# GpSimd instead of VectorE makes the four sums of each decoded w_out group

## The chip, the cores and the metric

The kernel runs on one core of one Trainium2 chip. The metric is the device time of one execution in microseconds (us), and the median of several executions is compared. The engines are called as the profile calls them: PE (TensorE matmuls) with PEld (its weight loads), DVE (VectorE), ACT (ScalarE), POOL (GpSimd) and SP (SyncE, which here only issues DMAs).

## The reference

Sigmoid attention over 8 batches, 12 heads, 448 positions and head size 64, and then a feed-forward layer with erf-gelu over the 3584 tokens (768 to 2048 to 768):

```python
scores = scale * np.matmul(q, k.transpose(0, 1, 3, 2)) - np.log(S)
attn = 1.0 / (1.0 + np.exp(-scores))
x = np.matmul(attn, v)          # then heads side by side: [3584, 768]
...
h = x @ w_in
g = 0.5 * h * (1.0 + erf(h * inv_sqrt2))
return (g @ w_out).astype(np.float32)
```

## The kernel before

**Arithmetic.** Both matrix products of the feed-forward layer are done by a Strassen-like scheme with 7 products of blocks instead of 8 (p = 1 to 7). Each fp32 operand is split in a high part (a rounded copy) and a low part (the rest), and each product is three matmuls: low weight with high operand, high with low, high with high (`terms`, L764). A weight is split by ACT (high, L321) and DVE (low, L328, in `low_to`). The operand of the first layer (x) is split by ACT (L811, L840 and others) and DVE (`combine`, L801, output `xl_p` or `x`); that of the second layer by ACT (L811) and DVE (L801, output `op`).

**Weights.** They are decoded from their memory layout in chunks by the class `Decoder`: ACT makes `me` from `raw` (L149, L160), DVE joins and rounds (`join` L179 and L187, `round` L193) into a tile `wd`. Sixteen chunks are of w_in, the last twelve of w_out; two chunks make one of six w_out groups (0 to 5). For each group `post` makes two sums (L217, L218) and stores five blocks to memory (L220), and `close` makes two differences (L228) and stores them (L229). Nineteen chunks are decoded during attention; the other nine, and all the group sums, fall into the beginning of the feed-forward part. A `wd` tile has two buffers, so the tile of group 2 takes the one of group 0, and its first `join` can only start when every store of group 0 has been read out:

```python
self.out = sb.tile([P, 4 * QUAD], F32, tag="wd", name=f"wd{i}", bufs=2)
```

The stored blocks come back as weight units: SP loads 128 x 768 pieces (`load_to`, L310) into four staging buffers `wst_all`, ACT and DVE split them into `whl`, of which there are four. A unit feeds 18 matmuls. There are 224 units: for each of four batch pairs b 28 of w_in and 28 of w_out.

**Order.** The schedule is written out by hand (`manual_schedule`): each engine runs its instructions in the order in which the program issues them. First comes attention; `last_pair` ends it and runs the decoder up to the sums of group 0. Then `ffn1` of b = 0 walks 56 items, two to a unit, in the order `IN_ORDER`: p = 1 and 2 (items 0 to 15), then 6, 7 and 4 (items 16 to 39), then 5 and 3 (40 to 55). Around each item it issues a share of the decoder's steps and, at fixed items, the splits of x, as the low part for p = 4 behind item 19, whose first user is item 21. `ffn2` of b = 0 follows, with the units of w_out in the order p = 1, 5, 2, 6, 3, 7, 4 and a split of `op` for each unit. `close` of a group is called at least five items after its `post`; for groups 4 and 5 it is called in `ffn2`.

**Queues.** POOL issues the stores of `wd` (L220, L229), the stores of attention's results (L604, L609) and the later loads of x (L353), one behind another in program order.

Of the kernel before, what the change touches and what calls it, by code (L numbers as in the profile page):

```python
# [15 lines left out]
ALU = mybir.AluOpType  # L16
# [6 lines left out]
def tile_sigmoid_attention_gelu_ffn(  # L23
# [10 lines left out]
    nc = tc.nc  # L34
# [69 lines left out]
    def mix(a, s):  # L104
        a11, a12, a21, a22 = a
        s1, s2, s3, s4 = s
        nc.vector.tensor_tensor(s1, a21, a22, op=ALU.add)
        nc.vector.tensor_tensor(s2, s1, a11, op=ALU.subtract)
        nc.vector.tensor_tensor(s3, a11, a21, op=ALU.subtract)
        nc.vector.tensor_tensor(s4, a12, s2, op=ALU.subtract)  # L110
        return {1: a11, 2: a12, 3: s4, 4: a22, 5: s1, 6: s2, 7: s3}
# [10 lines left out]
    def square(m):  # L122
        return m.rearrange("p (h f n) -> p h f n", h=2, f=2)

    class Decoder:
# [77 lines left out]
        def post(self):  # L203
            some = bool(self.mixing or self.pending and self.second)
            while self.mixing:
                j, a = self.mixing.pop()
                quads = [t[:, i * OP : i * OP + OP] for t in (a, self.mixed) for i in range(4)]
                parts = mix(quads[:4], quads[4:])
                for p in (1, 2, 4, 5, 6, 7, 3):
                    n = IN_ORDER.index((p, j))  # L210
                    nc.gpsimd.dma_start(scr_in[n // 2][:, n % 2], parts[p])
                self.done += 1
            while self.pending and self.second:
                (c, e), a = self.pending.pop(0)
                a11, a12, a21, a22 = (a[:, i * QUAD : i * QUAD + QUAD] for i in range(4))
                s2 = self.second(c * KE + e)
                nc.vector.tensor_tensor(a21, a21, a22, op=ALU.add)  # L217
                nc.vector.tensor_tensor(s2, a21, a11, op=ALU.subtract)  # L218
                for p, part in ((2, a12), (4, a22), (1, a11), (5, a21), (6, s2)):
                    nc.gpsimd.dma_start(scr_out[p, c][:, :, :, e], square(part))  # L220
                self.open.append((c, e, a12, a22, s2))
                self.groups += 1
            return some

        def close(self):
            c, e, a12, a22, s2 = self.open.pop(0)
            for p, part in ((3, a12), (7, a22)):
                nc.vector.tensor_tensor(part, part, s2, op=ALU.subtract)  # L228
                nc.gpsimd.dma_start(scr_out[p, c][:, :, :, e], square(part))  # L229
            self.closed += 1  # L230

# [534 lines left out]
    def feed_forward(banks):  # L766
# [110 lines left out]
        def ffn1(b, g, xs):  # L877
# [11 lines left out]
            for n, (p, j) in enumerate(IN_ORDER):  # L889
# [17 lines left out]
                if p == 1:  # L907
                    later.append(lambda g21=g21, ph=ph: nc.scalar.copy(g21, ph))  # L908
                elif p == 2:
                    later.append(lambda g11=g11, ph=ph: gelu(g11, ph))  # L910
                elif p == 6:
                    later.append(lambda g12=g12, ph=ph: nc.scalar.copy(g12, ph))
                elif p == 7:
                    later.append(lambda g22=g22, ph=ph: nc.scalar.copy(g22, ph))
                elif p == 4:
                    later.append(lambda g21=g21, ph=ph: gelu(g21, ph))
                else:
                    dst = g22 if p == 5 else g12
                    h = tmp()
                    combine(h, ph, dst, add)  # L920

                    def close(p=p, r=r, h=h, dst=dst, t1=g[0, 1][c], g11=g[0, 0][c]):
                        gelu(dst, h)
                        if p == 3 and r == 1:
                            later.append(lambda: combine(t1, t1, g11))

                    later.append(close)
# [181 lines left out]
```

## Time and profile before

| | |
|---|---|
| time, median of 3 runs | 1005.85 us (1005.49 to 1006.02) |
| profiled execution: time / span | 1007.21 us / 1005.4 us |
| PE busy | 1000.4 us of the span (99%), 6436 matmuls |
| DVE busy | 719.4 us (72%) |
| ACT busy | 678.2 us (67%) |
| POOL busy | 129.8 us (13%) |
| granted clock of PE | 1.0 of full speed in all 40 slices |

The span is the time from the first to the last instruction of the program; the profiled execution took 1.8 us more than it, and 1.4 us more than the median of the runs. Shares are means over stages: attention ends near 239 us, `ffn1` of b = 0 near 334 us, and the rest repeats four times with no decoding in it. Within 236 to 350 us DVE does the decoder's work beside the splits, and it is there that the change lies.

### The profile page before, as it was taken

The numbers are of one execution on the slowest core, as the hardware profiler recorded it, in microseconds if no ns is written. First come the engines' busy times: TensorE is split into PE (matmuls) and PEld (weight loads), VectorE is DVE, ScalarE is ACT, GpSimd is POOL, SyncE is SP. The second block draws the span as 40 slices with busy tenths as digits, with TensorE's granted clock in tenths as the row PEclk, the third lists the DMA queues.
The fourth block names the chain that finished last, engine by engine and source line by source line (L and its number), as shares of the span: only waits on it lengthen the run. The fifth ranks groups of instructions, "written<-read, shape, count | busy, mean of one in ns | idle before, by whom it ended". The sixth has DMA issues, their size and how long they took to land.

```text
span 1005.4 us, 16639 instructions
## 1 busy us (share of the span) xinstructions
PE 1000.4 (99%) x6436; PEld 901.1 (90%) x6436; DVE 719.4 (72%) x829; ACT 678.2 (67%) x942; POOL 129.8 (13%) x180
## 2 busy tenths in 40 slices
PE   9999999999999999999999999999999999999998
PEld 5665665566999999999999999999999999999998
DVE  3688888888988987764378877535887774378873
ACT  5788888789886665567665655766656467665653
POOL 0234444413223300010000000100000000000000
PEclk9999999999999999999999999999999999999999
DMA  9989999997996665563434446534444543334541
GB/s 270 269 278 337 360 353 348 364 311 264 350 328 212 204 220 145 174 212 126 138 111 131 149 138 190 183 111 137 126 118 147 167 147 115 111 110 126 143 138 67
DMA packets 82928, 199.18 MB, mean 198 GB/s; under 512 B 9120, under 2 KB 33984, under 8 KB 82848
## 3 DMA queue, kind: packets, MB, share of 16 engines
q1 hardware_dynamic: 69360, 152.24, 49.5%
q0 software_dynamic: 11552, 39.23, 11.2%
q10 hardware_dynamic: 1936, 6.63, 2.0%
q8 instruction: 51, 0.84, 0.3%
q14 instruction: 29, 0.24, 0.1%
HBM read 156.10 MB, written 41.29 MB: 196 GB/s over the span
## 4 chain that ended last, share of the span: by engine, by line
PE 93%; DMA 2%; DVE 2%; ACT 1%; issue 1%; DVEq 0%; ACTq 0%
PE pf L764 73%; PE pav L546 11%; PE sc L510 7%; PE sc_t L530 2%; DMA raw<-w_out_dram 1%; DMA wst_all<-scr_in 1%; DVE whl L328 1%; PE sc L498 1%; DMA qk<-k_dram 0%; ACT a_all L471 0%; DVE wd L179 0%; ACT me L149 0%; DVE x L608 0%; ACT whl L321 0%; DVE x L801 0%
## 5 line engine op out<-in xcount | busy, mean ns | idle before, releaser
L764 PE MATMUL pf<-op,whl 128*128 128x448 f32 (+1 forms) x2022 | 382.3, 352 | 0.0
L764 PEld LDWEIGHTS pf<-op,whl 128*128 128x128 f32 x2022 | 381.3, 189 | 0.5 <-DVE op L801 0.2
L764 PE MATMUL pf<-xh_p,whl 128*128 128x448 f32 x1296 | 353.2, 353 | 0.1
L328 DVE TENSOR_TENSOR whl<-wst_all,whl 128x768 fp32r<-128x768 f32 x224 | 213.7, 955 | 153.7 <-ACT whl L321 153.4
L321 ACT CAST whl<-wst_all 128x768 fp32r<-128x768 f32 x224 | 185.9, 830 | 142.7 <-PE pf L764 124.5
L764 PEld LDWEIGHTS pf<-xh_p,whl 128*128 128x128 f32 x1296 | 244.9, 189 | 1.6 <-issue 0.7
L764 PE MATMUL pf<-xl_p,whl 128*128 128x448 f32 x624 | 219.9, 352 | 0.0
L801 DVE TENSOR_TENSOR op<-g,op 128x896 fp32r<-128x896 f32 x112 | 121.5, 1086 | 0.9 <-ACT op L811 0.9
L764 PEld LDWEIGHTS pf<-xl_p,whl 128*128 128x128 f32 x624 | 117.9, 189 | 0.1
L811 ACT CAST op<-g 128x896 fp32r<-128x896 f32 x112 | 104.8, 936 | 1.7 <-PE pf L764 1.7
L546 PE MATMUL pav<-a_all,v 64*64 64x448 f32 x816 | 95.0, 539 | 0.0
L546 PEld LDWEIGHTS pav<-a_all,v 64*64 64x64 f32 x816 | 34.4, 133 | 42.0 <-issue 35.0
L801 DVE TENSOR_TENSOR g<-g,g 128x896 f32<-128x896 f32 x64 | 69.5, 1085 | 0.0
L798 ACT ACTIVATE g<-tmp 128x448 f32<-128x448 f32 x64 | 40.2, 630 | 38.1 <-DVE tmp L801 38.0
L798 ACT ACTIVATE g<-pf 128x448 f32<-128x448 f32 x64 | 34.7, 543 | 39.8 <-PE pf L764 39.5
L353 POOL DMA_DIRECT2D x<-scr_x x24 | 18.3, 815 | 324.5 <-ACT g L908 204.4
L471 ACT ACTIVATE a_all<-sc 128x896 f32<-128x896 f32 x64 | 55.5, 923 | 5.8 <-PE sc L498 3.5
L801 DVE TENSOR_TENSOR tmp<-pf,g 128x448 f32<-128x448 f32 x64 | 39.8, 623 | 26.2 <-PE pf L764 18.7
L546 PE MATMUL pav<-wst_all,v 64*64 64x448 f32 x272 | 55.3, 536 | 0.0
L471 ACT ACTIVATE a_all<-sc_t 128x896 f32<-128x896 f32 x24 | 22.1, 920 | 29.6 <-PE sc_t L530 29.6
L546 PE MATMUL pav<-a_lent,v 64*64 64x448 f32 x192 | 40.5, 537 | 0.0
L458 DVE TENSOR_TENSOR lo_all<-qk,hi_all 128x896 fp32r<-128x896 f32 x34 | 38.1, 1122 | 0.3
(106 smaller groups left out, 1023.2 us busy)
## 6 DMA issues: line engine op xcount, KB each, us to landing
wst_all<-scr_in SPq DMA_DIRECT2D x112, 384.0 KB, 3.2
wst_all<-scr_out SPq DMA_DIRECT2D x112, 384.0 KB, 3.1
v<-v_dram SPq DMA_DIRECT2D x48, 256.0 KB, 9.8
raw<-w_in_dram SPq DMA_DIRECT2D x16, 767.8 KB, 8.4
out_dram<-tmp SPq DMA_DIRECT2D x47, 224.0 KB, 2.1
qk<-q_dram SPq DMA_DIRECT2D x23, 448.0 KB, 9.2
qk<-k_dram SPq DMA_DIRECT2D x46, 224.0 KB, 9.2
scr_out<-wd POOLq DMA_DIRECT2D x36, 256.0 KB, 5.1
```

The lines of the kernel that those rows point to most:

```text
L321: nc.scalar.copy(hl[:, 0], t)
L328: nc.vector.tensor_tensor(hl[:, 1], t, hl[:, 0], op=ALU.subtract)
L353: queue.dma_start(dst[:, :, a], src[:, :, a])
L458: nc.vector.tensor_tensor(lo, raw, hi, op=ALU.subtract)
L471: nc.scalar.activation(to, sc, AF.Sigmoid, bias=NEG_LOG_S, scale=SCALE)
L510: nc.tensor.matmul(sc[:, j], ks[1][rows(j), keys], braid(qs[0][rows(j)]), start=n == 0, stop=n == 2,)
L530: nc.tensor.matmul(sc[rows(p), j], raw[rows(j), p, 1, FULL * P :], raw[rows(j), p, 0], start=True, stop=True,)
L546: nc.tensor.matmul(pav[rows(j), p], vals[u][half, p, j, c], a[p][half, j], start=not swap and c == order[0], stop=c == (order[-1], FULL - ...
L764: nc.tensor.matmul(bank, a, braid(m if half is None else straight(m)[:, half]), **flags)
L798: nc.scalar.activation(straight(dst), unbraid(src), AF.Gelu)
L801: nc.vector.tensor_tensor(out, a, b, op=op)
L811: nc.scalar.copy(op[:, 0], src)
```

## The change

The four additions and subtractions of each group, 24 in all, each 128 partitions x 512 fp32 elements with both inputs in SBUF, are issued on POOL instead of DVE:

```diff
                 s2 = self.second(c * KE + e)
-                nc.vector.tensor_tensor(a21, a21, a22, op=ALU.add)
-                nc.vector.tensor_tensor(s2, a21, a11, op=ALU.subtract)
+                nc.gpsimd.tensor_tensor(a21, a21, a22, op=ALU.add)
+                nc.gpsimd.tensor_tensor(s2, a21, a11, op=ALU.subtract)
                 for p, part in ((2, a12), (4, a22), (1, a11), (5, a21), (6, s2)):
                     nc.gpsimd.dma_start(scr_out[p, c][:, :, :, e], square(part))
...
             for p, part in ((3, a12), (7, a22)):
-                nc.vector.tensor_tensor(part, part, s2, op=ALU.subtract)
+                nc.gpsimd.tensor_tensor(part, part, s2, op=ALU.subtract)
                 nc.gpsimd.dma_start(scr_out[p, c][:, :, :, e], square(part))
```

On POOL, around the end of attention, the stores of group 0 stood behind two stores of attention's results (L609), with the sums elsewhere. Rows of before, in program order (`wd_2386` is the tile of group 0, `s_0` its second sum):

```order
L609 DMA scr_x<-x_0_2764 128x448
L609 DMA scr_x<-x_1_2767 128x448
L220 DMA scr_out_0_97<-wd_2386 512x1x128
L220 DMA scr_out_0_101<-wd_2386 512x1x128
L220 DMA scr_out_0_95<-wd_2386 512x1x128
L220 DMA scr_out_0_103<-wd_2386 512x1x128
L220 DMA scr_out_0_105<-s_0_2781 512x1x128
L609 DMA scr_x<-x_0_2810 128x448
L609 DMA scr_x<-x_1_2813 128x448
L229 DMA scr_out_0_99<-wd_2386 512x1x128
L229 DMA scr_out_0_107<-wd_2386 512x1x128
```

The same place of POOL's program now, without the middle of the stores:

```order
L609 DMA scr_x<-x_1_2767 128x448
L217 ISA
L217 TENSOR_TENSOR wd_2386<-wd_2386 128x512
L218 TENSOR_TENSOR s_0_2781<-wd_2386 128x512
L220 DMA scr_out_0_97<-wd_2386 512x1x128
...
L609 DMA scr_x<-x_1_2813 128x448
L228 TENSOR_TENSOR wd_2386<-wd_2386,s_0_2781 128x512
L229 DMA scr_out_0_99<-wd_2386 512x1x128
L228 TENSOR_TENSOR wd_2386<-wd_2386,s_0_2781 128x512
L229 DMA scr_out_0_107<-wd_2386 512x1x128
L217 TENSOR_TENSOR wd_2594<-wd_2594 128x512
```

Every store of a group now stands behind its sums on POOL, and there is one row that the source does not name: `L217 ISA`, which the built program calls a reload of GpSimd's library of routines (index 0). It stands once, ahead of the first sum.

On DVE, in the first items of `ffn1`, the rows around the first `join` of group 2 (`wd_2975`) change like this (`wd_2594` is the tile of group 1, `whl` the weight units, `xl_p` a low part of x):

```order
 L801 TENSOR_TENSOR xl_p_2955<-x_p_2614,xh_p_2893 128x1344
-L217 TENSOR_TENSOR wd_2594<-wd_2594 128x512
-L218 TENSOR_TENSOR s_1_2967<-wd_2594 128x512
 L179 SCALAR_TENSOR_TENSOR wd_2975<-raw_2544,me_2927 128x1024
```

What is left of DVE's program keeps its order, so a low part (L328) that stood behind a `join` still stands behind it. ACT, SP and PE have the same rows in the same order.

## Rows read from the trace of the kernel before

**Rows 1.** The page: busy time of PE, and its granted clock by slice.
```profile
PE 1000.4 (99%) x6436; PEld 901.1 (90%) x6436; DVE 719.4 (72%) x829; ACT 678.2 (67%) x942; POOL 129.8 (13%) x180
...
PEclk9999999999999999999999999999999999999999
```

**Rows 2.** Timeline of PE: first matmul of the feed-forward part (start, length, instruction).
```profile
238.55 0.46 PE L764 MATMUL pf<-xh_p,whl 128*128 128x448 f32 x1
```

**Rows 3.** The chain that ended last: its longest piece (start, length).
```profile
269.57 732.80 PE pf L764 x3876
```

**Rows 4.** Stretches of 5 us: busy PE, PEld, DVE, ACT, POOL; clock; DMA share; GB/s.
```profile
240.00:245.00 5.00, 5.00 (x28) 5.00 (x27) 5.00 (x6) 4.97 (x9) 1.55 (x3) 1.00 1.01 352
...
255.00:260.00 5.00, 5.00 (x28) 5.00 (x27) 4.97 (x6) 4.17 (x7) 0.00 (x0) 1.00 1.00 348
```

**Rows 5.** Timeline of DVE, 253 to 274 us; in brackets idle time before.
```profile
253.46 1.22 DVE L179 SCALAR_TENSOR_TENSOR wd<-raw,me 128x1024 uint32<-128x1024 uint32 x1
...
255.39 0.94 DVE L328 TENSOR_TENSOR whl<-wst_all,whl 128x768 fp32r<-128x768 f32 x1
...
269.12 0.96 DVE L328 TENSOR_TENSOR whl<-wst_all,whl 128x768 fp32r<-128x768 f32 x1 [1.18 <-ACT whl L321]
...
271.86 1.55 DVE L801 TENSOR_TENSOR xl_p<-x,xh_p 128x1344 fp32r<-128x1344 f32 x1
```

**Rows 6.** Timeline of DVE, 306 to 338 us.
```profile
306.69 1.23 DVE L179 SCALAR_TENSOR_TENSOR wd<-raw,me 128x1024 uint32<-128x1024 uint32 x1 [2.04 <-DMA scr_out<-wd]
...
323.23 0.62 DVE L801 TENSOR_TENSOR tmp<-pf,g 128x448 f32<-128x448 f32 x1
...
336.97 1.09 DVE L801 TENSOR_TENSOR op<-g,op 128x896 fp32r<-128x896 f32 x1
```

**Rows 7.** Timeline of PEld around 338 us.
```profile
338.12 0.49 PEld L764 LDWEIGHTS pf<-op,whl 128*128 128x128 f32 x3 [0.20 <-DVE op L801]
```

**Rows 8.** Timeline of POOL at the end of attention.
```profile
235.63 1.11 POOL L609 DMA_DIRECT2D scr_x<-x  x2 [13.38 <-DVE x L608]
236.73 2.97 POOL L220 DMA_DIRECT2D scr_out<-wd  x4
239.27 1.18 POOL L220 DMA_DIRECT2D scr_out<-s  x1
```

**Rows 9.** Groups of DVE instructions by line and shape: count, busy us, mean ns.
```profile
L228 DVE TENSOR_TENSOR wd<-wd,s 128x512 f32<-128x512 f32 x12 | 7.7, 684 | 0.0
...
L218 DVE TENSOR_TENSOR s<-wd 128x512 f32<-128x512 f32 x6 | 4.2, 692 | 0.2
L217 DVE TENSOR_TENSOR wd<-wd 128x512 f32<-128x512 f32 x6 | 4.1, 685 | 0.0
```

**Rows 10.** Groups of POOL instructions: its only one that reads SBUF and computes.
```profile
L447 POOL CAST hi_all<-qk 128x896 fp32r<-128x896 f32 x30 | 31.9, 1068 | 21.6 <-DMA qk<-k_dram 12.5 <-PE sc L510 9.1
```

**Rows 11.** Timeline of DVE at two places where a cast of POOL overlaps it.
```profile
60.58 2.27 DVE L458 TENSOR_TENSOR lo_all<-qk,hi_all 128x896 fp32r<-128x896 f32 x1
...
62.84 1.08 DVE L458 TENSOR_TENSOR lo_all<-qk,hi_all 128x896 fp32r<-128x896 f32 x1
...
205.05 1.09 DVE L475 COPY wst_all<-sc 128x896 f32<-128x896 f32 x1
206.05 1.74 DVE L193 CUSTOM_DVE_ANT_0 wd<-raw,wd 128x2048 uint16<-128x2048 uint16 x1
```

**Rows 12.** Timeline of POOL at the same two places.
```profile
60.95 0.94 POOL L447 CAST hi_all<-qk 128x896 fp32r<-128x896 f32 x1
...
204.84 1.88 POOL L447 CAST hi_all<-qk 128x896 fp32r<-128x896 f32 x2 [2.78 <-DMA qk<-k_dram]
```

**Rows 13.** Stores of `post` (L220): issue to landing.
```profile
DMA to landing us min/median/max: 2.7/6.0/9.3
```

**Rows 14.** Stores of `close` (L229): issue to landing.
```profile
DMA to landing us min/median/max: 2.7/4.5/8.6
```

**Rows 15.** Timeline of ACT: the trace's only load of an engine's function table.
```profile
240.06 1.28 ACT L1060 ACT_TABLE_LOAD   x1
```

## The prediction

> **What bounds the kernel now.** I read the page first: PE is busy 1000.4 of 1005.4 us, at full granted clock in every slice [rows 1]. So the time is PE's work plus PE's stalls, and the change touches no matmul. Next, how regularly PE runs: the feed-forward part begins at 238.55 us [rows 2] and its last long piece ends at 269.57 + 732.80 = 1002.37 us [rows 3]. 763.8 us over 224 weight units is 3.41 us a unit, 1.705 us an item. This gives each operand a due time: unit i starts at 238.55 + 3.41 i. Then the stretch in which the moved sums lie: PE does not stop, but DVE is busy 5.00 and 4.97 of 5 us, and the DMA engines are full [rows 4]. DVE is not the bound, but it runs just ahead of it. Last, how far ahead, from DVE's timeline. The low part of unit 6 (L328 at 255.39) ends at 256.33 and is due at 259.0: 2.7 us early [rows 5]. The low part of x for p = 4 (L801 at 271.86) ends at 273.41; its first user is the second matmul of item 21, at 238.55 + 21 x 1.705 + 0.2 = 274.6: little over 1 us early [rows 5]. The low part of `op` for the second unit of `ffn2` (336.97 to 338.06) is not early at all: PE's weight load waits 0.20 us for it [rows 6, 7]. At two places, then, about a microsecond of lateness on DVE becomes time of the kernel, and there is next to nothing to gain.
>
> **The change part by part.**
>
> *What leaves DVE.* 24 instructions, 7.7 + 4.2 + 4.1 = 16.0 us of busy time [rows 9], 0.67 us each. It helps PE only where DVE is late: at the end of `ffn1`, by the 0.20 us of [rows 7].
>
> *What a sum costs on POOL.* No POOL sum is in the trace. The nearest row is POOL's cast, 896 elements a partition in 0.94 us when undisturbed [rows 12], 1.07 in the mean [rows 10]. A sum of 512 elements reads 2 x 512 = 1024. Reading its inputs together at the cast's rate it would take 0.94 x 512 / 896 = 0.54 us; as two casts, 1.9 us. I take the reading as what counts: 0.94 x 1024 / 896 = 1.1 us.
>
> *Contention.* At 60.95 us a cast starts on POOL during a DVE subtraction with two SBUF inputs [rows 11, 12]. The cast keeps its 0.94 us and the subtraction takes 2.27 instead of the 1.08 of its next instance. At 206.05 DVE's L193 ends 1.07 us after the cast that overlaps it (ends 206.72) and takes 1.74 us, while the copy from PSUM before it (L475, 1.09 us) is not slowed [rows 11, 12]. So a POOL instruction that reads SBUF costs a two-input DVE instruction its whole length, and one that reads PSUM nothing. [...] I count 1.1 us of DVE time for each POOL sum beside two-input work, and about 0.4 us that POOL waits for the DVE instruction in progress (half of a usual 0.9).
>
> *The library row.* `L217 ISA` stands ahead of POOL's first sum, behind two stores that wait for attention's last results until 235.63 [rows 8], so it can start at 236.7 and nothing hides it on POOL. The trace has no such load. Below, the nearest is ACT's table load, 1.28 us [rows 15]. [...] I take R = 9 us, as the stretch is the fullest. [...]
>
> *Group 0 on POOL.* Reload from 236.7 to 245.7. Two sums of 1.1 + 0.4: 248.7. Five stores at (239.27 - 236.73) / 4 = 0.63 us each [rows 8]: 251.9. Two L609 stores, 1.1 us [rows 8]: 253.0. L228 overwrites a block whose store must have been read out; issued at 248.7, it lands at 254.7 by the median [rows 13]. Sum 255.8, its store's issue 256.4, second sum 257.5; this last store lands 4.5 us later [rows 14], at 262.0. In all 253.0 + R.
>
> *What waits for it.* The tile of group 2 is that of group 0, so the `join` of 253.46 [rows 5] can't start before 262.0: 8.5 us late. DVE comes to it earlier than before (six sums less ahead of it), so it only waits. Queued behind it on DVE are L187, the low part of unit 6, L193 and everything later; ACT's load of the next `raw` waits in its turn for that L193, with ACT's later work behind it. Unit 6's low part ends at 256.33 + 8.5 = 264.9 instead of being due at 259.0: a first PE stall of 5.9 us. From the `join` to the end of x's low part were 273.41 - 253.46 = 19.95 us. Less 1.18 idle and four sums of 0.67, 16.1 remain; plus four POOL sums in that stretch (both differences of group 1, both sums of group 2; group 1's first two run while DVE waits), 4.4. That is 282.5, against 274.6: PE is then **8.0 us late, or R - 1.0**. This contains the first stall.
>
> After that DVE has idle gaps again, and the tiles of the later groups come free in time, since POOL closes a group right behind its stores, and no longer where DVE reached it. Even the 2.04 us that DVE waited for such a store at 306.69 [rows 6] should go.
>
> *The end of ffn1.* Six POOL sums (group 5's two, then the differences of 4 and 5) now run ahead of 336.97: 6.6 us. About every second DVE instruction there is a `tmp` that reads PSUM, as at 323.23 [rows 6]; a POOL sum can run under one, 0.53 us of issue pace: 3.2 covered, 3.4 left. Against it stand two sums removed (1.3) and the wait of 2.04 that went. That leaves 0.1; with the 0.2 of today **0.3 us**. Ends: -0.2 if all is hidden, +3.3 without cover. The five stores of group 5 stand behind its sums, about 2.5 us later; their units are loaded well before PE needs them, so I cost that at nothing; without that cover it is those 2.5 us.
>
> *Sum.* 8.0 + 0.3 = 8.3 us. The span becomes 1013.7, the profiled execution 1015.5; on the median, which lies 1.4 us under the profiled execution, **1014.2 us**.
>
> **The rivals.**
>
> *Not slower: the reload is short.* With R = 1.3, a table load's price, the chain on POOL ends at 254.3, within a microsecond of the old start of the `join`; the stall is R - 1.0 = 0.3, and with the end of `ffn1` the time is 1006.5. It decides at R of about 2.7: below it the loss stays within 0.2%, 2 us, which is about what a measurement of this kernel can tell. For it: the row has no operands and waits for nothing. [...] A gain beyond 0.2% would need 2 us of stalls to remove, and the whole PE row has none after 270 us that I could find but the 0.20.
>
> [...]
>
> *Sums dearer.* At 1.9 us each, 0.8 more, four of them lengthen group 0's chain and four DVE's stretch: 6.4 us more; at the end of `ffn1` six: 4.8 more. With R = 9 that gives 1025.4, with R = 1.3 still 1017.7. For it: DVE loses 1.19 us to a cast of 0.94, so handing over costs as well. Against: the sum reads hardly more than the cast.
>
> **How the numbers follow.** The forecast's mechanism (reload of about 5 to 12 us, then the tile of group 0) has 0.62 and gives 1010 to 1017.5. The short reload has 0.18, of which 0.01 is a gain; the long one 0.12; dear sums 0.08. The range 1007 to 1019 holds the forecast, part of the short reload (whose upper half lies above 1007) and of the long one: about 8 in 10. Slower by over 0.2% (above 1007.9): 0.62 + 0.12 + 0.08 = 0.82; within 0.2%: 0.17; faster: 0.01.
>
> **What would show it.** The reload: POOL's first sum starts near 246 instead of 237, with nothing on POOL in between. The tile: DVE idle for many microseconds ahead of the `join`, released by a store of `wd`. The stall: PE idle near 259 and again before item 21, some 8 us in all, and DVE, ACT and PE running in step again by 300. The contention: two-input DVE instructions that last about 1 us longer beside POOL's sums, and sums of 1.1 to 1.5 us. The end of `ffn1`: the wait before the second `op` unit stays below 1 us. The prediction is wrong if POOL's first sum starts by 239, if the `join` doesn't wait, or if PE's stalls lie at the end of `ffn1` instead.

## The result, and the profile after

The changed kernel takes 1017.36 us (median of 4 runs, 1017.06 to 1017.88), the kernel before 1005.81 us (4 runs, 1005.49 to 1006.02): 11.55 us more, a ratio of 1.011 (95% interval 1.0097 to 1.0122). The profiled execution took 1017.88 us, its span is 1016.1 us, 10.7 more than before (less than 11.55, as the profiled execution lay 1.4 us above the median before and 0.5 after). The forecast was 1014.2 us, in a range of 1007 to 1019. The sign and the range held, but by luck: the trace shows that the largest term of the sum did not occur and that others, set too small, took its place.

The page after, busy time by engine and granted clock; it answers to [rows 1]:

```profile
PE 1005.7 (99%) x6436; PEld 903.9 (89%) x6436; DVE 729.8 (72%) x805; ACT 678.3 (67%) x942; POOL 169.4 (17%) x204
...
PEclk9999999999999899999999999999999999999999
```

DVE has 24 instructions less and is busy 10.4 us longer. The 24 cost 16.0 us [rows 9], so what was left of DVE's program grew by 10.4 + 16.0 = 26.4 us: 1.10 us for each sum on POOL. The groups by line and shape show where (columns as in [rows 9]), first before:

```profile
L328 DVE TENSOR_TENSOR whl<-wst_all,whl 128x768 fp32r<-128x768 f32 x224 | 213.7, 955 | 153.7 <-ACT whl L321 153.4
...
L801 DVE TENSOR_TENSOR xl_p<-x,xh_p 128x1344 fp32r<-128x1344 f32 x15 | 23.3, 1556 | 6.0 <-ACT xh_p L824 6.0
...
L179 DVE SCALAR_TENSOR_TENSOR wd<-raw,me 128x1024 uint32<-128x1024 uint32 x12 | 14.6, 1220 | 5.8 <-ACT me L160 3.8 <-DMA scr_out<-wd 2.0
...
L187 DVE TENSOR_SCALAR raw<-raw 128x1024 uint32<-128x1024 uint32 x12 | 8.5, 710 | 0.4
```

and after:

```profile
L328 DVE TENSOR_TENSOR whl<-wst_all,whl 128x768 fp32r<-128x768 f32 x224 | 226.8, 1014 | 155.8 <-ACT whl L321 155.4
...
L801 DVE TENSOR_TENSOR xl_p<-x,xh_p 128x1344 fp32r<-128x1344 f32 x15 | 24.4, 1629 | 6.0 <-ACT xh_p L824 6.0
L179 DVE SCALAR_TENSOR_TENSOR wd<-raw,me 128x1024 uint32<-128x1024 uint32 x12 | 18.5, 1542 | 3.8 <-ACT g L798 2.2 <-ACT me L160 1.6
...
L187 DVE TENSOR_SCALAR raw<-raw 128x1024 uint32<-128x1024 uint32 x12 | 10.9, 906 | 0.4
```

L328 makes 13.1 of the 26.4 us and L179 3.9. Not all of it has two SBUF inputs: the shift L187 has one, and makes 2.4.

POOL's timeline at the end of attention, the place of [rows 8]:

```profile
235.97 1.11 POOL L609 DMA_DIRECT2D scr_x<-x  x2 [13.37 <-DVE x L608]
237.18 1.28 POOL L217 TENSOR_TENSOR wd<-wd 128x512 f32<-128x512 f32 x1
238.54 1.88 POOL L218 TENSOR_TENSOR s<-wd 128x512 f32<-128x512 f32 x1
240.37 2.95 POOL L220 DMA_DIRECT2D scr_out<-wd  x4
```

The first sum starts 0.1 us behind the stores: the reload that was to take 9 us takes no more than that. A sum lasts 1.28 us here; the next one lasts 1.88; it begins while a low part of DVE (L328 at 236.98, 2.31 us long) is in progress, so it probably waits for that one. The instructions of L217 and L228 by line (count, then the shortest, median and longest in ns, then the first and last start), with the two rows of POOL's sequencer that stand under the same line, just ahead of the first sum:

```profile
L217 POOL TENSOR_TENSOR wd<-wd x6: 1275/1916/3395, 237.2 to 325.5; 128x512 f32<-128x512 f32 x6
L217 POOLq MODIFY_POOL_CONFIG  x2: 33/35/37, 237.1 to 237.1; - x2
...
L228 POOL TENSOR_TENSOR wd<-wd,s x12: 1273/1362/1790, 245.1 to 339.3; 128x512 f32<-128x512 f32 x12
```

PE's stalls in order of time, each with what released it:

```profile
238.89 0.46 PE L764 MATMUL pf<-xh_p,whl 128*128 128x448 f32 x1
...
260.39 0.46 PE L764 MATMUL pf<-xh_p,whl 128*128 128x448 f32 x1 [0.49 <-DVE whl L328]
267.83 0.46 PE L764 MATMUL pf<-xh_p,whl 128*128 128x448 f32 x1 [0.36 <-ACT pf L885]
272.51 0.46 PE L764 MATMUL pf<-xh_p,whl 128*128 128x448 f32 x1 [1.01 <-ACT g L912]
278.30 0.46 PE L764 MATMUL pf<-xl_p,whl 128*128 128x448 f32 x1 [0.22 <-DVE xl_p L801]
...
316.41 0.46 PE L764 MATMUL pf<-xh_p,whl 128*128 128x448 f32 x1 [0.57 <-DVE tmp L801]
...
337.44 0.46 PE L764 MATMUL pf<-xh_p,whl 128*128 128x448 f32 x1 [2.00 <-DVE tmp L801]
342.10 0.74 PE L764 MATMUL pf<-xh_p,whl 128*128 128x448 f32 x1 [1.57 <-DVE tmp L801]
```

To add up a stall with what it costs around it, I compare when the same weight load starts in the two traces and call the difference PE's lag. It is 0.34 us at the start of the feed-forward part (238.89 against [rows 2]), 3.44 us after 280, 4.28 after the stall of 316, and 10.67 us from 350 to the end. So the change costs 3.1 us early, 0.8 at 316 and 6.4 at the end of `ffn1`, and nothing behind that: the last long piece of the chain now begins at 342.10 and lasts 670.94 us, against [rows 3].

### The profile page after: what moved, and what is told of

The parts are those of the page before. It is cut to its first block, busy times and chain, and to the rows that moved or that the text cites. A ratio compares the mean times of both kernels' runs of the same rounds, so it can differ in the third digit from the quotient of the medians.

```text
span 1016.1 us, 16640 instructions
## 1 busy us (share of the span) xinstructions
PE 1005.7 (99%) x6436; PEld 903.9 (89%) x6436; DVE 729.8 (72%) x805; ACT 678.3 (67%) x942; POOL 169.4 (17%) x204
## 4 chain that ended last, share of the span: by engine, by line
PE 87%; DMA 5%; DVE 5%; issue 2%; ACT 1%; SPq 0%; POOL 0%; DVEq 0%; ACTq 0%; POOLq 0%
PE pf L764 69%; PE pav L546 10%; PE sc L510 7%; DMA qk<-k_dram 3%; PE sc_t L530 1%; DVE whl L328 1%; DMA raw<-w_in_dram 1%; DVE wd L179 1%; DMA wst_all<-scr_in 1%; DVE tmp L801 1%; DVE xl_p L801 0%; DVE x L801 0%; DVE op L801 0%; DVE x L608 0%; DVE raw L187 0%
## 5 line engine op out<-in xcount | busy, mean ns | idle before, releaser
L328 DVE TENSOR_TENSOR whl<-wst_all,whl 128x768 fp32r<-128x768 f32 x224 | 226.8, 1014 | 155.8 <-ACT whl L321 155.4
## 6 DMA issues: line engine op xcount, KB each, us to landing
raw<-w_in_dram SPq DMA_DIRECT2D x16, 767.8 KB, 8.2
```

The costliest lines, as they stand in the source:

```text
L328: nc.vector.tensor_tensor(hl[:, 1], t, hl[:, 0], op=ALU.subtract)
```

## The experiments

Each time stands beside the kernel before on the same chip: 1005.65 us in the first four runs, 1006.12 in the next three, 1006.15 in the last two. "Feed-forward" is the time from PE's first to its last matmul on a weight unit in the trace: 763.8 us before, 774.1 after. "Lost" is the difference to the kernel before by the medians.

| run | what is on GpSimd | time, us | ratio (95%) | lost | feed-forward |
|---|---|---|---|---|---|
| the change | all 24 sums | 1017.36 | 1.011 (1.0097 to 1.0122) | 11.55 | 774.1 |
| e3_memset | 72 memsets instead | 1007.57 | 1.0024 (1.0014 to 1.0035) | 1.9 | 765.0 |
| e6_dummy | 20 unused sums, none moved | 1021.07 | 1.0151 (1.0136 to 1.0167) | 15.4 | 779.0 |
| e4_first4 | groups 0 to 3 | 1010.00 | 1.0044 (1.0027 to 1.006) | 4.4 | 767.8 |
| e5_last2 | groups 4 and 5 | 1011.34 | 1.0056 (1.0041 to 1.0071) | 5.7 | 769.4 |
| e1_post | L217 and L218 | 1010.06 | 1.004 (1.0025 to 1.0055) | 3.9 | 767.1 |
| e2_close | L228 | 1011.88 | 1.0058 (1.0041 to 1.0075) | 5.8 | 769.5 |
| e8_switch | all 24, another library before | 1025.08 | 1.019 (1.0174 to 1.0205) | 19.0 | 781.1 |
| e9_late_dve | all but L228 of groups 4, 5 | 1011.32 | 1.005 (1.0035 to 1.0065) | 5.2 | 767.7 |
| e10_late_pool | L228 of groups 4, 5 | 1009.63 | 1.0032 (1.0017 to 1.0047) | 3.5 | 767.1 |

**Reading or queue?** Since the 9 us of the reload did not occur, the theory became: a GpSimd sum that reads SBUF holds up DVE's instructions with two SBUF inputs (by 1.10 us each in the mean, from the busy times above), and DVE's lateness reaches PE. The expectations call this the theory of the port; that is a name alone, since the runs show lengths and no port. The rival: the sums delay the stores behind them on POOL's queue, and the `wd` tiles come free late. The first run keeps POOL as long busy, but with nothing read:

```diff
-                nc.gpsimd.tensor_tensor(a21, a21, a22, op=ALU.add)
-                nc.gpsimd.tensor_tensor(s2, a21, a11, op=ALU.subtract)
+                for part in (a21, a21, a21, s2, s2, s2):
+                    nc.gpsimd.memset(part, 0.0)
...
-                nc.gpsimd.tensor_tensor(part, part, s2, op=ALU.subtract)
+                for _ in range(3):
+                    nc.gpsimd.memset(part, 0.0)
```

> Each of the 24 sums is replaced by three GpSimd memsets of the same tile: GpSimd is as long in the way of its own stores, but reads no SBUF. The sums are left out, so the products with w_out have wrong operands. Theory of the port (each GpSimd sum takes about 1.1 us from a VectorE instruction with two SBUF inputs): VectorE's instructions keep their lengths and it does 16 us less, so 1005.3 to 1006.5 us, no PE stall at the end of ffn1. Rival of the queue (stores stand behind the sums, land later, and tiles and weight units come late): stores are as late as in the changed kernel, so 1014 to 1018 us.

The second adds sums whose result nothing uses, to the kernel before, for groups 1 to 5:

```diff
+                if c * KE + e:
+                    spare = first_sum(0)
+                    self.spare = spare
+                    for _ in range(2):
+                        nc.gpsimd.tensor_tensor(spare, a11, a21, op=ALU.add)
                 for p, part in ((2, a12), (4, a22), (1, a11), (5, a21), (6, s2)):
...
+            if c * KE + e:
+                for _ in range(2):
+                    nc.gpsimd.tensor_tensor(self.spare, a12, a22, op=ALU.add)
```

> The kernel before, with its sums on VectorE, and 20 extra GpSimd sums of two SBUF inputs whose results nobody uses: two behind the stores of each post and two behind those of each close, for groups 1 to 5. Theory of the port: VectorE keeps its 16 us and loses some 22 more, so slower than before by 6 to 11 us, 1012 to 1017 us. Rival of the queue: every store stands ahead of the extra sums of its own group, so 1005.5 to 1008 us.

With the memsets 1.9 us are lost by the medians, 1.4 to 3.5 by the interval, and in the trace the feed-forward part is 1.2 us longer against 10.3 for the change. So the queue has a small share, though the time lies 1.1 us above the range of the theory. The run also takes the 16.0 us of the sums off DVE, so it can't say what late stores cost beside a full DVE; the part on the end of `ffn1` below shows one place. DVE's splits in that run (line numbers are one higher) are as short as before, though POOL is as busy as after (169.7 us):

```profile
L329 DVE TENSOR_TENSOR whl<-wst_all,whl 128x768 fp32r<-128x768 f32 x224 | 213.7, 955 | 159.9 <-ACT whl L322 159.5
```

```profile
L229 POOL MEMSET wd<- 128x512 f32 x36 | 22.0, 611 | 4.2 <-DMA scr_out<-wd 2.8
L218 POOL MEMSET wd<- 128x512 f32 x18 | 9.6, 532 | 21.8 <-DVE wd L193 21.2
```

With the 20 unused sums DVE executes the same 829 instructions as before and is busy 742.0 us instead of 719.4, 22.6 / 20 = 1.13 us a sum; the kernel loses 15.4 us, which lies above the 1012 to 1017 us expected and far from the rival's. Reading, much more than the queue, is what costs: DVE's split of a weight has a mean of 981 ns in the run with the unused sums, which read SBUF, and 955 ns in the run with the memsets, which only write it and leave it at the 955 of before.

**Which groups?** Both runs are the change with the engine chosen by group:

```diff
+                eng = nc.gpsimd if (c * KE + e) < 4 else nc.vector
+                eng.tensor_tensor(a21, a21, a22, op=ALU.add)
+                eng.tensor_tensor(s2, a21, a11, op=ALU.subtract)
...
+                eng.tensor_tensor(part, part, s2, op=ALU.subtract)
```

> Groups 0 to 3 make their sums on GpSimd, groups 4 and 5 on VectorE as before. Theory of the port: the early loss of 3 us stays, plus at most 1.5 at the end of ffn1, where VectorE comes in late but no GpSimd sum runs: 1008.5 to 1010.5 us, PE at full clock throughout. Rival (the loss at the end of ffn1 comes from lateness carried in from the first groups): 1014 to 1017 us.

> Only groups 4 and 5 make their sums on GpSimd. Theory of the port: no early loss; six GpSimd sums ahead of the second op unit of ffn2 take about 0.97 us each from VectorE, 5.9 in all, less 1.3 for the two sums removed: 4.5 us and a little for the clock, 1010 to 1011.5 us. Rival (lateness carried in): 1005.8 to 1007.5 us.

Both lie in their ranges, 1010.00 and 1011.34. With groups 0 to 3, PE's lag grows by 2.9 us up to 276 and by 1.0 behind it. With groups 4 and 5, the lag is flat up to 327 and then grows by 5.9. So the two losses are separate, and the two halves by themselves add up to 4.4 + 5.7 = 10.1 of the 11.55 us. The other 1.4 us come only when both stand together; no run says why.

**Which sums?** The change with its other part undone, L228 in the first run, L217 and L218 in the second:

```diff
-                nc.gpsimd.tensor_tensor(part, part, s2, op=ALU.subtract)
+                nc.vector.tensor_tensor(part, part, s2, op=ALU.subtract)
```

```diff
-                nc.gpsimd.tensor_tensor(a21, a21, a22, op=ALU.add)
-                nc.gpsimd.tensor_tensor(s2, a21, a11, op=ALU.subtract)
+                nc.vector.tensor_tensor(a21, a21, a22, op=ALU.add)
+                nc.vector.tensor_tensor(s2, a21, a11, op=ALU.subtract)
```

> Only the two sums of each group (L217, L218) are on GpSimd; the two differences (L228) are on VectorE as before. Theory (a GpSimd sum holds up VectorE's two-input work by about 1.1 us, and VectorE's lateness reaches TensorE at two places): of the losses of the whole change, about 3 us early and 6.4 us at the end of ffn1, the early one stays in part (the six early sums of groups 0 to 2) and at the end only group 5's two run ahead of the op split, 2.2 us against 1.3 us taken from VectorE; so 1007.5 to 1010 us, VectorE busy near 719.4 - 8.3 + 12 x 1.1 = 724 us. Rival (the stores wait behind the sums on GpSimd's queue and the decoder's tile comes free late): the five stores behind each pair of sums are all still late, so nearly the whole loss stays, 1014 to 1017 us.

> Only the two differences of each group (L228) are on GpSimd; its two sums are on VectorE as before. Theory (VectorE held up by 1.1 us per GpSimd sum): the four differences of groups 4 and 5 now run ahead of the op split at the end of ffn1, where in the kernel before they stood behind it on VectorE: 4.4 us there with nothing taken away ahead of it, and about 1 to 2 us early: 1010 to 1013 us, VectorE busy near 719.4 - 7.7 + 12 x 1.1 = 725 us. Rival (stores late behind sums on GpSimd's queue): the five stores of each group are issued as early as before, only the last two of each group stand behind a sum, so little is lost: 1006 to 1008 us. With the run of the sums alone on GpSimd it should add up to about the change's 11.5 us.

1010.06 us lies just above the theory's range and far from the rival's 1014; 1011.88 is in the theory's range. Together they lose 3.9 + 5.8 = 9.7 us. DVE is busy 725.6 us with the differences on POOL (13.9 / 12 = 1.16 us each) and 720.7 with the sums there (9.6 / 12 = 0.80, where 1.1 had been expected), so the sums of `post` are the cheaper half for DVE. In time there may be a second reason, their order: POOL makes the last four differences earlier than DVE did.

**The order at the end of ffn1.** In the kernel before, DVE makes the differences of groups 4 and 5 behind the `op` split of 336.97 [rows 6]; POOL makes them ahead of it. Two runs move only these four, back to DVE in the change, and to POOL in the kernel before:

```diff
+                eng = nc.gpsimd if (c * KE + e) < 4 else nc.vector
-                nc.gpsimd.tensor_tensor(part, part, s2, op=ALU.subtract)
+                eng.tensor_tensor(part, part, s2, op=ALU.subtract)
```

(in the second run `>= 4` in place of `< 4`, with L217 and L218 on DVE).

> The changed kernel, with the four differences of groups 4 and 5 alone back on VectorE, where they stand behind the op split of the second ffn2 unit. Theory (the loss at the end of ffn1 is those four differences, which GpSimd makes ahead of that split, 1.1 to 1.2 us of VectorE each; group 5's two sums cost no more than they take away): 4.5 to 5 us of the 11.5 come back, 1012 to 1013.5 us, and the stretch of VectorE from group 5's first join to the end of that split is again 31.4 us long instead of 36.5. Rival (it is VectorE's lateness carried in from earlier, the late tile of group 5, that stalls TensorE there): less than 2 us come back, 1015.5 us or more.

> The kernel before, with the four differences of groups 4 and 5 alone on GpSimd. Theory (as for the run that puts them back): the same stretch of VectorE grows from 31.4 to about 36 us, and the time by 4 to 5 us, to 1009.8 to 1011 us, although only 4 of the 24 instructions have moved. Rival (they hurt only where VectorE is already late): under 2 us lost, below 1008 us.

DVE's timeline gives the stretch that decides it, from group 5's first `join` (L179) to the end of the second `op` split. After the change:

```profile
311.53 1.23 DVE L179 SCALAR_TENSOR_TENSOR wd<-raw,me 128x1024 uint32<-128x1024 uint32 x1 [2.18 <-ACT g L798]
...
332.11 2.53 DVE L801 TENSOR_TENSOR op<-g,op 128x896 fp32r<-128x896 f32 x1
334.56 0.61 DVE L801 TENSOR_TENSOR tmp<-pf,g 128x448 f32<-128x448 f32 x1
335.10 1.75 DVE L328 TENSOR_TENSOR whl<-wst_all,whl 128x768 fp32r<-128x768 f32 x1
336.77 0.61 DVE L801 TENSOR_TENSOR tmp<-pf,g 128x448 f32<-128x448 f32 x1
337.31 2.00 DVE L801 TENSOR_TENSOR g<-g,g 128x896 f32<-128x896 f32 x1
...
346.90 1.08 DVE L801 TENSOR_TENSOR op<-g,op 128x896 fp32r<-128x896 f32 x1
```

The same two ends with the four differences back on DVE:

```profile
309.02 1.23 DVE L179 SCALAR_TENSOR_TENSOR wd<-raw,me 128x1024 uint32<-128x1024 uint32 x1 [2.04 <-ACT g L799]
...
339.43 1.08 DVE L802 TENSOR_TENSOR op<-g,op 128x896 fp32r<-128x896 f32 x1
```

And with only these four on POOL:

```profile
304.60 1.22 DVE L179 SCALAR_TENSOR_TENSOR wd<-raw,me 128x1024 uint32<-128x1024 uint32 x1 [1.83 <-DMA scr_out<-wd]
...
338.73 1.08 DVE L802 TENSOR_TENSOR op<-g,op 128x896 fp32r<-128x896 f32 x1
```

Before, the stretch is 336.97 + 1.09 - 306.69 = 31.4 us. After it is 36.5, with the four back on DVE 31.5, with only these four on POOL 35.2. So the four make 3.8 to 5.0 us of it, and group 5's two sums cost no more than they took away. In time, putting them back recovers 11.55 - 5.17 = 6.4 us, more than the 4.5 to 5 expected (1011.32, just below its range); moving them alone costs 3.5 us, just below what was expected (1009.63). Both rivals fall: four of 24 instructions make 3.5 to 6.4 of the 11.55 us.

**Where the reload went.** One unused GpSimd instruction of another library, first in the program:

```diff
+        nc.vector.memset(ones[:, 4:6], 0.0)
+        nc.gpsimd.partition_broadcast(ones[:, 6:8], ones[:, 4:6], channels=P)
```

> The changed kernel, with one early GpSimd instruction of another library (a broadcast of two columns within the tile of ones, whose result nothing uses) ahead of everything else, so that the library which the sums need is no longer the last one loaded when the L217 ISA row comes. Theory A (the row costs nothing because in the changed kernel the library is already resident; a switch would cost what the prediction feared, R of 6 to 12 us): the first sum starts 6 to 12 us after the stores of L609 instead of 0.1 us after them, and the time rises by R - 1, to 1022 to 1028 us. Theory B (the row costs nothing in any case, or the load is done ahead of its turn): the first sum starts within 1 us of the stores and the time stays at 1017 to 1018.5 us.

Theory A held, at 1025.08 us. POOL's timeline at the end of attention, with the same two rows of the sequencer ahead of the sum:

```profile
234.67 1.11 POOL L609 DMA_DIRECT2D scr_x<-x  x2 [13.38 <-DVE x L608]
243.61 1.66 POOL L217 TENSOR_TENSOR wd<-wd 128x512 f32<-128x512 f32 x1 [7.82 <-PE pf L766]
```

```profile
L217 POOLq MODIFY_POOL_CONFIG  x2: 37/37/37, 235.9 to 235.9; - x2
```

The sequencer's rows take 33 to 37 ns in the two kernels; what differs is the time from them to the sum, 7.7 us here against 0.1 in the changed kernel (the matmul named as releaser has nothing to do with it). At the program's start 7.0 us lie between the same rows at 1.0 and the broadcast at 8.03. The chain that the prediction described now runs: DVE's `join` of group 2 waits 10.81 us for a store of group 0's tile, and PE stalls 9.32 us for the low part of unit 6.

```profile
262.07 1.23 DVE L179 SCALAR_TENSOR_TENSOR wd<-raw,me 128x1024 uint32<-128x1024 uint32 x1 [10.81 <-DMA scr_out<-wd]
```

```profile
267.61 0.74 PE L766 MATMUL pf<-xh_p,whl 128*128 128x448 f32 x1 [9.32 <-DVE whl L328]
```

In this kernel PE's lag grows by 13.4 us early, by 1.2 near 319 and by 2.7 at the end of `ffn1`, 17.3 in all. The granted clock was 0.50 from 265 to 270 us, and behind the stall, up to 273.4, PE's lag grew by 2.9 us without a wait. This isn't time on top of DVE's lateness: at 287.34 PE waits for DVE again, 1.13 us for the low part of x.

A third buffer for `wd`, which would have taken the wait on the tile away by itself, wasn't tried.

## Why the prediction was right in sign and wrong in its terms

By the signs that it named itself, the prediction's mechanism was wrong: POOL's first sum starts before 239, at 237.18, the `join` doesn't wait, and the longest stalls of PE lie at the end of `ffn1`. The time came out near all the same, because 8.0 us that did not occur were replaced by 3.1 us early and by 7.2 us from 280 on, where 0.3 had been counted. That is luck.

**What bounds the kernel.** Right: PE's stalls lie at the two places named, up to item 21 and at the end of `ffn1`, and nothing is given back. Two of the early ones name ACT (267.83 and 272.51). ACT was late through DVE, by a route that the prediction doesn't have: DVE's low part that frees a staging buffer ended at 252.78, 2.9 us later than before, and ACT then waited for the load into that buffer. A row of the chain that ended last, and one of ACT's timeline:

```profile
252.80 7.97 DMA wst_all<-scr_in
```

```profile
260.84 0.83 ACT L321 CAST whl<-wst_all 128x768 fp32r<-128x768 f32 x1 [3.77 <-DMA wst_all<-scr_in]
```

**What leaves DVE, and what a sum costs it.** Right: 16.0 us leave, and each sum costs DVE 1.10 us in the mean, as counted. That the two agree is partly luck: 1.1 us was the length assumed for a sum, but a sum takes 1.27 to 1.37 us undisturbed, and its cost to DVE was 0.80 us for the sums of `post` and 1.16 for the differences where each ran alone, and 0.97 at the end of `ffn1`.

**The library row.** This step failed: "I take R = 9 us, as the stretch is the fullest". No run shows 9 us, nor that a full stretch lengthens a reload; that was the author's estimate. In its place the runs showed 0.1 us from the stores to the first sum in the changed kernel, and 7.8 us (243.61 - 235.78) with an instruction of another library at the start. That the library was already in place in the changed kernel is theory A's explanation, which fits both; no row shows it directly. The mechanism behind it was right, as the run with the other library shows: there POOL's first sum, the tile, DVE (10.81 us) and PE (9.32 us) wait for each other as described. Its size was too small there too, 13.4 us of early lag against "R - 1.0" = 6.8. From POOL's first sum to the `join` that run takes 262.07 - 243.61 = 18.5 us, where the prediction has 262.0 - 245.7 = 16.3, mostly since the last store lands 6.1 us after its issue instead of 4.5. From the `join` to the end of x's low part it takes 25.2 us instead of 20.5: POOL makes six sums in that stretch and not four, and DVE waits 1.38 us for ACT. Together 6.9 us more. The rival of the short reload had the condition right, though not its time of 1006.5. (A slip of the sum: R = 12 gives 1017.2, not 1017.5.)

**Group 0 and what waits for it.** With R near 0 that formula gives no stall, but 3.1 us were lost early. The formula let the sums ahead of the `join` run "while DVE waits". Without the wait they run beside DVE's own work. Ten sums stand ahead of the end of x's low part: 10 x 1.10 = 11.0 us added, 10 x 0.67 = 6.7 removed, 4.3 us late. Measured: that end moves from 273.41 [rows 5] to 276.69 + 1.55 = 278.24, less the 0.34 of the start 4.5 us. The slack of little over 1 us leaves 3.3; PE's lag grew by 3.1. The `join` itself doesn't wait for the tile; it starts at 257.20, 3.7 us later than before:

```profile
254.64 2.63 DVE L801 TENSOR_TENSOR xl_p<-x_p,xh_p 128x1344 fp32r<-128x1344 f32 x1
257.20 1.21 DVE L179 SCALAR_TENSOR_TENSOR wd<-raw,me 128x1024 uint32<-128x1024 uint32 x1
...
276.69 1.55 DVE L801 TENSOR_TENSOR xl_p<-x,xh_p 128x1344 fp32r<-128x1344 f32 x1
```

**The end of ffn1.** The second failed step: 0.3 us predicted, 6.4 measured, or 7.2 with the 0.8 at 316, by two terms. First, "a POOL sum can run under one, 0.53 us of issue pace: 3.2 covered, 3.4 left": next to nothing was covered. In the stretch of DVE shown above, the instructions beside POOL's six sums are 5.8 us longer than before, 0.97 a sum; less the two sums removed (1.4), and with 0.5 us that DVE waits for PE, that is 4.9 of the 5.1 us by which the stretch is longer. A `tmp` lasts 0.61 us as before and a sum 1.3, so each sum reaches into a two-input neighbour: the `op` split at 332.11 takes 2.53 us instead of 1.09. (The 0.3 also holds the 0.2 us stall of [rows 7], which the time before has already.)

Second, "Even the 2.04 us that DVE waited for such a store at 306.69 [rows 6] should go": it went where only the differences moved (e2_close: that `join` starts at 306.50 without idle time, although PE is 2.4 us late there, and the last store of its tile is issued at 296.03), but not in the change. With the sums on POOL, all five stores of a group stand behind them, and the first difference of group 3 waits 2.51 us for the store of the block that it overwrites. The last store is issued 3.0 us later than before, within PE's own lag of 3.4 us:

```profile
300.93 1.30 POOL L228 TENSOR_TENSOR wd<-wd,s 128x512 f32<-128x512 f32 x1 [2.51 <-DMA scr_out<-wd]
302.53 0.73 POOL L229 DMA_DIRECT2D scr_out<-wd  x1 [0.30 <-POOL wd L228]
303.21 1.36 POOL L228 TENSOR_TENSOR wd<-wd,s 128x512 f32<-128x512 f32 x1
304.87 0.73 POOL L229 DMA_DIRECT2D scr_out<-wd  x1 [0.30 <-POOL wd L228]
```

The two stores of L229 in this stretch then land 5.9 and 7.0 us after their issue, where the same two took 3.3 and 4.5 before (shortest, median, longest, after the change):

```profile
DMA to landing us min/median/max: 5.9/6.5/7.0
```

The core moved 410 and 396 GB/s in the two stretches of 5 us from 300 us on, against 253 GB/s from 301 to 306 us before, which may be the reason; no run tests it. The `join` at 311.53 still waits 2.18 us, and is 311.53 - 306.69 - 3.44 = 1.4 us later against PE than before, where 2.0 us of gain were counted. (Its row names an ACT instruction that ended 0.2 us earlier; the landing lies 0.7 us earlier. Which of them released the last 0.7 us isn't settled.) So the rival of the queue has a share here, this 1.4 us. 5.1 + 1.4 = 6.5 us of lateness, against 7.2 of lag from 280 us on. The stalls at the end of `ffn1` are the sign that the prediction named for this.

**The price on PE.** PE's stalls there name `tmp`, not `op`: `tmp` empties the PSUM tile that PE writes next, and stands behind the held-up instructions on DVE. The prediction priced only the weight load that waits for `op`.

**The rivals.** "Sums dearer" with a short reload came to 1017.7, next to the measured time, but not by its mechanism: the sums cost DVE 1.10 us each in the mean and not more; there were more of them on the path.

## What to carry to other kernels

In these runs work moved from VectorE to GpSimd was not taken off VectorE, where both read SBUF: 0.67 us left and 1.10 us came back, for each of 24 instructions. Count each moved instruction on every path that it can now run ahead of, since another engine's queue may make it earlier than its old place in the order; four that came earlier cost 3.5 to 6.4 us. A reload in GpSimd's program says little of time by itself: the same row cost 0.1 us here, and 7.8 us with one early instruction of another library.

## What the runs showed of the hardware that was not expected

TensorE's granted clock fell from 1.00 to 0.51 after the stalls at the end of `ffn1`. By stretches of 5 us (columns as in [rows 4]):

```profile
335.00:340.00 5.00, 3.00 (x12) 2.42 (x10) 5.00 (x6) 2.08 (x4) 4.40 (x5) 0.81 0.92 269
340.00:345.00 5.00, 3.43 (x10) 2.62 (x9) 4.97 (x6) 4.55 (x7) 4.70 (x7) 0.51 0.74 208
345.00:350.00 5.00, 5.00 (x28) 5.00 (x27) 4.50 (x6) 3.26 (x5) 2.75 (x4) 1.00 0.99 338
```

Behind the stall of 2.00 us that ended at 337.44 the granted clock is 0.81 in the first of these stretches and 0.51 in the second, and from 345 us on it is 1.00 again. A stall's length alone did not decide it: e2_close has a stall of 2.1 us, released by ACT, and a mean clock of 1.000. Little of the loss comes from the clock, since PE waits for DVE in any case: the `op` split that ends the lateness starts 346.90 - 336.97 = 9.9 us later than before, against a final lag of 10.7, which leaves 0.8 us. DVE itself waited 0.52 us for the slower PE just ahead of that split, so by these rows the clock cost about 1.3 us at most:

```profile
345.50 0.63 DVE L801 TENSOR_TENSOR tmp<-pf,g 128x448 f32<-128x448 f32 x1 [0.52 <-PE pf L764]
```

Memsets on GpSimd, which only write, left DVE's two-input instructions alone (the split of a weight 955 ns and the `op` split 1084 ns, against 955 and 1086 before), but not all of DVE: the 128 x 1024 shift of the decoder (L187, one SBUF input) had a mean of 771 ns beside them, against 710 before. Beside sums, which read as well, it was 906 ns after the change and 1080 ns with the 20 unused sums. So this one-input work on DVE was not safe from POOL either. With the memsets:

```profile
L187 DVE TENSOR_SCALAR raw<-raw 128x1024 uint32<-128x1024 uint32 x12 | 9.3, 771 | 0.4
```
